# Attention and two feed-forward layers on one core: weight conversion by a leaky activation, and three changes of the plan

## The chip, the cores and the metric

The kernel runs on 1 core of one Trainium2 chip. The metric is device time in microseconds (us) of one execution, median of several runs.

## The reference, cut to what matters

```python
# q, k, v: (8 batches, 8 heads, 576 tokens, 64), float32
k_p = k.reshape(B, H, 72, 8, D).mean(axis=3)      # pooled by 8
v_p = v.reshape(B, H, 72, 8, D).mean(axis=3)
attn = softmax(q @ k_p.T / sqrt(64))
x = (attn @ v_p) as (4608 tokens, 512)
# first feed-forward: w_in 512 x 2048, w_out 2048 x 512
h = x @ w_in
g = (a0 + a1*h + a2*h**2 + a3*h**3) / (1 + |b0|*|h| + |b1|*h**2 + 1e-6)
x = g @ w_out
# second feed-forward: w_gate, w_val 512 x 1536, w_out2 1536 x 512
out = (sigmoid(x @ w_gate) * (x @ w_val)) @ w_out2
```

All weights arrive as float64. The kernel sees each as two 32-bit words, and must make float32 of them itself.

## The kernel before, in words

Every float32 product of a weight and an activation is made of three matmuls: both factors are split into a high and a low part (`wh`, `wl`, `xh`, `xl`), and `mm3` (lines 485 to 487) adds wl\*xh, wh\*xh and wh\*xl in one PSUM bank.

**Blocks and steps.** The 4608 tokens are cut into 9 blocks of 512. The first feed-forward is a loop of 144 steps: step n is block n // 16 and slice n % 16 of the 2048 hidden columns. A step computes `hidden` (`g1`, 12 matmuls), the rational function (`rational1` to `rational3`), the split of its result (`split_g`, of the step before), and the second product (`g2`, 12 matmuls, of three steps before, `LAG`), which adds into the four banks `acc0` to `acc3`. After a block's last `g2`, `g2_out` (line 561) copies the four banks to SBUF and stores them in DRAM as `x2d`. The second feed-forward begins after step 143; the change doesn't touch it.

**Attention.** While block b of the loop runs, the attention of block b+1 is done in the gaps, in tiles of 128 tokens or of 64 where a batch ends (4 or 5 tiles in a block; block 1 has 5). Block 0 is done ahead of the loop. A planner (lines 430 to 470) gives each piece a step and a place in it: `scores`, `exponential` and `normalise`, `a_transpose`, `attend`, and, for each batch, pooling of keys (`pool_k`, VectorE) and of values (`pool_v`, GpSimd), `place_k` and `mask_v`. `at[i]` is the step of tile i. For blocks from 2 on (`late_`), the transposes stand in step `at[i]` and `attend` one step later; for block 1, the transposes stand in step `at[i] - 1`, one step after `normalise`, and `attend` in `at[i]`. Every engine runs its instructions in the order written, so this plan fixes each queue.

**Conversion of weights.** `conv1a` (line 84) makes two ScalarE copies per slice of 128x512 weights: the high word, read as float32, times 2\*\*-112 (line 90), and the low word times 2\*\*-29 (line 92). `conv1b` (line 94), which `gap()` starts one step later between `rational2` and `rational3`, does the rest: VectorE shifts the high word left by 3 into a spare tile `wx` (line 98), VectorE puts the sign bit back with a scalar_tensor_tensor (line 100), and GpSimd adds the low word (line 102). `conv2` splits the result: ScalarE rounds it (line 117), and the rest is a subtraction (line 118), on GpSimd in all calls. `weights_a(n)` does this for `w_in` and `w_out`, a slice of each per step, ahead of the loop and in block 0.

**Weights of the second feed-forward.** `background(n - 16)` (line 194) prepares them from block 1 on, in 12 units of 8 steps: two loads and one more, three conversions (`conv1` at r = 2, 3 and 6), four GpSimd subtractions (line 214), seven splits (`bg_split`, lines 190 and 191) and one `conv2`, and stores them in DRAM (`w2d`, `wo2d`). The 12 units fill blocks 1 to 6; block 7 has no background work.

**PSUM.** Four banks (tag "h") rotate among `hidden`, the scores, the transposes and `attend`. Four more are `acc0` to `acc3`.

The step's order, in short, as each engine's queue gets it:

```python
g1(n); run(on_pe, n, 0); rational1(n); run(off_pe, n, 0); split_g(n - 1)
rational2(n); run(off_pe, n, 2); gap(); rational3(n); g2(m); g2_out(m)
run(on_pe, n, 1); run(off_pe, n, 1); weights_a(n) or wo_stream; background(n - NF1)
```

VectorE's six instructions of a step are lines 528 to 530 (`rational1`) and 542 to 544 (`rational3`). Lines 528 and 544, and the two of `conv1b`, read and write SBUF tiles alone; lines 529, 530, 542 and 543 read the PSUM bank `h`.

Of the kernel before, what the change touches and what calls it, by code (L numbers as in the profile page):

```python
# [9 lines left out]
F32 = mybir.dt.float32  # L10
F32R = mybir.dt.float32r
I32 = mybir.dt.int32
U32 = mybir.dt.uint32
AF = mybir.ActivationFunctionType
ALU = mybir.AluOpType
# [20 lines left out]
def attention_moe_glu_kernel(ctx: ExitStack, tc: tile.TileContext, q, k, v, w_in, w_out, ca, cb, w_gate, w_val, w_out2, out):  # L36
    nc = tc.nc
# [8 lines left out]
    NJ = H // 2  # L46
    NF1, NF2 = F1 // P, F2 // P
    TB = 512
    NB = NT // TB
    NTT = TB // P  # L50
    NCH = (H * SP + P - 1) // P
# [10 lines left out]
    scale = 1.0 / math.sqrt(D)  # L62
# [13 lines left out]
    def new_tmp(name, tag="m", bufs=3):  # L76
        return rot.tile([P, 512], F32, tag=tag, name=name, bufs=bufs)

    x2d = [dram.tile([P, NJ, TB], F32, name=f"x2d{i}", tag=f"x2d{i}") for i in range(NB)]
# [4 lines left out]
    def conv1a(*raws):  # L84

        for raw in raws:
            hw, lw = raw[:, :, 1], raw[:, :, 0]


            nc.scalar.activation(hw.bitcast(F32), hw.bitcast(F32), AF.Copy, scale=2.0 ** -112)  # L90

            nc.scalar.activation(lw, lw.bitcast(U32), AF.Copy, scale=2.0 ** -29)

    def conv1b(*raws):

        ws = [(raw[:, :, 1], raw[:, :, 0], new_tmp("wx").bitcast(I32)[:, :raw.shape[1]]) for raw in raws]
        for hw, lw, x in ws:
            nc.vector.tensor_scalar(out=x, in0=hw, scalar1=3, scalar2=None, op0=ALU.logical_shift_left)
        for hw, lw, x in ws:
            nc.vector.scalar_tensor_tensor(out=hw, in0=hw, scalar=-2 ** 31, in1=x, op0=ALU.bitwise_and, op1=ALU.bitwise_or)  # L100
        for hw, lw, x in ws:
            nc.gpsimd.tensor_tensor(out=hw, in0=hw, in1=lw, op=ALU.add)

    between = []
# [1 line left out]
    def conv1(*raws):  # L106
        conv1a(*raws)
        between.append(lambda: conv1b(*raws))
# [6 lines left out]
    def conv2(raw, wh, wl, eng=nc.gpsimd):  # L115
        t = raw[:, :, 1].bitcast(F32)
        nc.scalar.activation(wh, t, AF.Copy)
        eng.tensor_tensor(out=wl, in0=t, in1=wh.bitcast(F32), op=ALU.subtract)
# [7 lines left out]
    def slot(tag, dtype, name, pool=None):  # L126
        shape = [P, 2, 4 * P] if dtype is F32R else [P, 4 * P, 2]
        return (pool or wp).tile(shape, dtype, tag=tag, name=name)
# [8 lines left out]
    wi, wo, wi_raw, wo_raw = {}, {}, {}, {}  # L137
# [10 lines left out]

    def wi_conv2(f):
        wi[f] = slot(f"wi{f}", F32R, "wi")  # L150
        conv2(wi_raw.pop(f), wi[f][:, 0], wi[f][:, 1])

    def wo_load(f):
        wo_raw[f] = slot(f"wo{f + 1}", I32, "woraw") if f + 1 < FS else slot(f"st{(f + 1 - FS) % 5}", I32, "woraw", stage)
# [38 lines left out]

    def background(n):

        if not 0 <= n < 8 * NF2:
            return
        u, r = divmod(n, 8)
        s_, mat = divmod(u, 2)
        if r == 0:  # L200
            bg.setdefault("out", 0)
            bg["raw"] = [slot(f"st{x}", I32, "wqraw", stage) for x in range(3)]
            for x in range(2):
                f = 2 * s_ + x
                load_raw(bg["raw"][x], (w_gate, w_val)[mat][:, 2 * f * P:2 * (f + 1) * P], True)
            load_raw(bg["raw"][2], w_out2[u * P:(u + 1) * P, :], False)
        elif r in (2, 3):
            conv1(bg["raw"][r - 2])
        elif r == 4:
            b1, b2 = (raw[:, :, 1].bitcast(F32) for raw in bg["raw"][:2])  # L210
            b11, b21, b12, b22 = b1[:, :2 * P], b1[:, 2 * P:], b2[:, :2 * P], b2[:, 2 * P:]
            t = stage.tile([P, 4, 2 * P], F32, tag="st3", name="wqt")
            for o, a, b in ((0, b12, b11), (1, b22, t[:, 0]), (2, b22, b12), (3, b21, t[:, 1])):
                nc.gpsimd.tensor_tensor(out=t[:, o], in0=a, in1=b, op=ALU.subtract)
            bg["op"] = {1: b11, 2: b21, 3: b22, 4: t[:, 3], 5: t[:, 0], 6: t[:, 1], 7: t[:, 2]}
        elif r == 5:
            bg_split(u, 0)
            bg_split(u, 2)
        elif r == 6:
            conv1(bg["raw"][2])  # L220
            bg_split(u, 4)
        elif r == 7:
            bg_split(u, 6)
            t = slot(f"st{4 + bg['out'] % 2}", F32R, "wq", stage)
            bg["out"] += 1
            conv2(bg["raw"][2], t[:, 0], t[:, 1])
            nc.sync.dma_start(wo2d[u], t.bitcast(F32).rearrange("p h x -> p (h x)"))

    with tc.manual_schedule():
# [29 lines left out]
        units, raws, loaded = [], {}, [0]  # L259
# [168 lines left out]


        of_block, first, last = {}, {}, {}  # L430
        SH = (1, 3)
        for i, (b, t0, n) in enumerate(tiles):
            of_block.setdefault((b * S + t0) // TB, []).append(i)
            first.setdefault(b, i)
# [1 line left out]
        at = {}  # L436
        for blk, idx in of_block.items():
            for m, i in enumerate(idx):
                at[i] = NF1 * (blk - 1) + SH[blk == 1] + m * (NF1 - (0, 1)[blk == 1] - SH[blk == 1]) // len(idx) if blk else m - len(idx)
        plan = []  # L440
        n0 = len(of_block[0])

        def put(step, rank, pe, rest, gen, *a, use=()):
            plan.append((step, rank, len(plan), pe, rest, gen(*a), use))

        for i, (b, t0, n) in enumerate(tiles):
            late_ = at[i] > NF1
            put(at[i] + late_, 0, 0, 0, attend, i)
            if late_:
                put(at[i], 2, 0, 0, a_transpose, i)  # L450
            else:
                put(at[i] - 1, 2, 1, 1, a_transpose, i)
            put(at[i] - 2, 3, 0, 0, exponential, i)
            put(at[i] - 2, 3, 1, 1, normalise, i)
            put(at[i] - 3, 4, 1, 1, scores, i, use=[("q", i)])
# [6 lines left out]
        for b in range(1, B):  # L462
            e0, e1 = max(at[first[b - 1]], -2), at[last[b - 1]]
            for c in range(2 * NCH):
                w, f = (("k", pool_k), ("v", pool_v))[c // NCH]
                st = e0 + c * (e1 - 3 - e0) // (2 * NCH)
                put(st, 6, 1, 1 if st < 0 else 2, ew, f, b, c % NCH, use=[(w, b, c % NCH)])
            put(e1 - 2, 3.5, 1, 1, ew, place_k, b)
            put(e1 + (e1 > NF1), 1, 0, 0, ew, mask_v, b)
        plan.sort(key=lambda x: (x[0], (0, 2, 1)[x[4]], x[1], x[2]))  # L470
        units += [u for x in plan for u in x[6]]
        lead = plan[0][0]
# [23 lines left out]
        acc, gs = {}, {}  # L496
# [4 lines left out]
        def store(a, dst, on_act, *tag):  # L501
            o = new_tmp("o", *tag)
            if on_act:
                nc.scalar.activation(o, a, AF.Copy)
            else:
                nc.vector.tensor_copy(o, a)
            nc.sync.dma_start(dst, o)
# [53 lines left out]
        def g2_out(n):  # L561
            i, f = divmod(n, NF1)
            if f == NF1 - 1:
                for e in range(NJ):
                    store(acc[i][e], x2d[i][:, e], e < 2, *(("su", 3) if e == NJ - 1 else ()))


        ring, wo2, xo = {}, {}, {}
# [201 lines left out]
        for n in range(N1):  # L770
            m = n - LAG
# [23 lines left out]
            x = n - (N1 - NF1)  # L795
# [79 lines left out]
```

## Time and profile before

| | us |
|---|---|
| median of 3 runs | 1896.74 (1896.67 to 1898.65) |
| the profiled execution, its own time | 1894.58 |
| its span, first to last instruction | 1892.7 |

Read the page first for the share of each engine, then the stretches by block, then the chain that ended last within a stretch, and only then single instructions. A block's stretch is cut at the first `hidden` matmul of the block: 36.2 us for block 0, 195.3 for block 1, 302.4, 415.3, 525.0, 637.7, 744.0, 855.3 for blocks 2 to 7, and 957.1 for block 8. PE is TensorE, DVE VectorE, ACT ScalarE, POOL GpSimd, SP the engine whose queue issues the DMAs. The row of a stretch has its two ends, its length, then the busy time (and count of instructions) of PE, PEld (weight loads), DVE, ACT and POOL, TensorE's mean granted clock, DMA share and GB/s. A busy time in these views runs from the start to the end of an instruction and holds any time in which it stood still; successive instructions of an engine overlap a little.

### The profile page before, as it was taken

Reading aid. Unit: us, or ns where it says so; the run is one execution under the profiler, and the core shown is the slowest. Engines: PE = TensorE matmul, PEld = TensorE weight load, DVE = VectorE, ACT = ScalarE, POOL = GpSimd, SP = SyncE. Lnnn points to the kernel's source line nnn. Section 1 sums busy time; section 2 is a strip of 40 time slices with the busy share of each in tenths; the row PEclk is TensorE's granted clock in tenths of the full one; section 3 lists DMA queues with packets and bytes.
Section 4 is the critical chain, followed back from the end, with each engine's and each line's share of the span. In section 5 each row is a group of like instructions: output and inputs, shape, how many; then the busy total and the mean of one; then the engine's idle time right before and its main releaser. Section 6 shows DMA issues by size and latency. Waiting matters only on the chain.

```text
span 1892.7 us, 25138 instructions
## 1 busy us (share of the span) xinstructions
PE 1804.6 (95%) x8936; PEld 1564.4 (83%) x8936; DVE 1242.5 (66%) x1847; ACT 943.0 (50%) x1754; POOL 896.4 (47%) x855
## 2 busy tenths in 40 slices
PE   5578999999999999999999999999999999999999
PEld 4467788787777788788887999998998998998997
DVE  7999999999998899988778543343334333333331
ACT  4777777677676777776666422222222222222221
POOL 6768556565564665653224234334235225235231
PEclk9799999999999999999999999999999999999999
DMA  7343355343544553443154574574573664663661
GB/s 247 131 153 120 107 191 187 135 171 135 186 159 156 192 176 137 168 148 119 56 196 150 190 236 153 166 235 133 184 228 123 211 211 129 222 201 112 206 203 43
DMA packets 123117, 312.56 MB, mean 165 GB/s; under 512 B 11504, under 2 KB 43248, under 8 KB 122992
## 3 DMA queue, kind: packets, MB, share of 16 engines
q1 hardware_dynamic: 122992, 310.95, 48.7%
q8 instruction: 71, 1.16, 0.2%
q14 instruction: 54, 0.44, 0.1%
HBM read 257.95 MB, written 52.95 MB: 164 GB/s over the span
## 4 chain that ended last, share of the span: by engine, by line
PE 67%; DVE 21%; ACT 4%; issue 4%; DMA 2%; POOL 2%; SPq 0%; ACTq 0%; POOLq 0%; DVEq 0%
PE h L485 13%; PE h L487 12%; PE h L486 12%; PE acc L485 3%; PE acc L487 3%; PE acc L486 3%; PE accA L722 3%; PE accA L723 3%; PE h L722 3%; PE h L723 3%; PE accA L721 3%; PE h L721 3%; DVE u L528 3%; PE psx L413 3%; DVE y L544 3%
## 5 line engine op out<-in xcount | busy, mean ns | idle before, releaser
L658 DVE TENSOR_TENSOR t<-h,t 128x384 f32<-128x384 f32 x360 | 200.7, 557 | 387.0 <-ACT t L666 276.2
L513 POOL TENSOR_TENSOR g<-y,g 128x512 fp32r<-128x512 f32 x144 | 190.6, 1324 | 245.7 <-ACT g L510 186.7
L711 POOL TENSOR_TENSOR t<-t 128x384 f32<-128x384 f32 x72 | 84.4, 1172 | 448.9 <-issue 253.7
L485 PE MATMUL h<-xs,wi 128*128 128x512 f32 x576 | 234.4, 407 | 11.8 <-DVE xs L420 5.2
L485 PE MATMUL acc<-g,wo 128*128 128x512 f32 x576 | 232.8, 404 | 2.2 <-ACT g L510 2.2
L487 PE MATMUL h<-xs,wi 128*128 128x512 f32 x576 | 229.3, 398 | 3.0 <-DVE xs L420 3.0
L486 PE MATMUL h<-xs,wi 128*128 128x512 f32 x576 | 229.2, 398 | 0.0
L487 PE MATMUL acc<-g,wo 128*128 128x512 f32 x576 | 226.0, 392 | 2.4 <-POOL g L513 2.4
L486 PE MATMUL acc<-g,wo 128*128 128x512 f32 x576 | 225.0, 391 | 0.0
L487 PE MATMUL h<-xS,wq 128*128 128x384 f32 x576 | 193.1, 335 | 0.0
L485 PE MATMUL h<-xS,wq 128*128 128x384 f32 x576 | 192.9, 335 | 0.0
L486 PE MATMUL h<-xS,wq 128*128 128x384 f32 x576 | 192.7, 335 | 0.0
L528 DVE SCALAR_TENSOR_TENSOR u<-s,coef,u 128x512 f32<-128x512 f32 x144 | 132.1, 918 | 32.2 <-ACT u L526 31.9
L485 PE MATMUL h<-xA,wq 128*128 128x384 f32 x432 | 149.0, 345 | 0.0
L544 DVE SCALAR_TENSOR_TENSOR y<-u,y 128x512 f32<-128x512 f32 x144 | 143.9, 999 | 4.9
L487 PE MATMUL h<-xA,wq 128*128 128x384 f32 x432 | 144.7, 335 | 0.0
L486 PE MATMUL h<-xA,wq 128*128 128x384 f32 x432 | 144.6, 335 | 0.0
L485 PEld LDWEIGHTS h<-xs,wi 128*128 128x128 f32 x576 | 111.3, 193 | 39.1 <-DVE xs L420 4.2
L525 ACT ACTIVATE s<-h 128x512 f32<-128x512 f32 x144 | 85.0, 590 | 110.4 <-PE h L487 110.3
L542 DVE SCALAR_TENSOR_TENSOR u<-u,h 128x512 f32<-128x512 f32 x144 | 98.5, 684 | 56.0 <-ACT h L538 54.3
L487 PEld LDWEIGHTS h<-xs,wi 128*128 128x128 f32 x576 | 111.1, 193 | 27.9 <-DVE xs L420 3.5
L485 PEld LDWEIGHTS acc<-g,wo 128*128 128x128 f32 x576 | 108.5, 188 | 27.9 <-ACT g L510 2.6
(122 smaller groups left out, 4300.2 us busy)
## 6 DMA issues: line engine op xcount, KB each, us to landing
wq<-w2d SPq DMA_DIRECT2D x252, 512.0 KB, 4.3
wo<-wod SPq DMA_DIRECT2D x88, 512.0 KB, 3.8
w2d<-wq SPq DMA_DIRECT2D x36, 512.0 KB, 2.9
x2d<-o SPq DMA_DIRECT2D x36, 256.0 KB, 2.4
out_dram<-o SPq DMA_DIRECT2D x36, 256.0 KB, 2.0
raw<-in_k_dram SPq DMA_DIRECT2D x32, 256.0 KB, 2.8
raw<-in_q_dram SPq DMA_DIRECT2D x32, 256.0 KB, 2.7
raw<-in_v_dram SPq DMA_DIRECT2D x32, 256.0 KB, 3.1
```

What stands on the lines that cost most here:

```text
L485: nc.tensor.matmul(out_, wl, xh, start=start, stop=False, skip_group_check=on)
L486: nc.tensor.matmul(out_, wh, xh, start=False, stop=False, skip_group_check=on)
L487: nc.tensor.matmul(out_, wh, xl, start=False, stop=stop, skip_group_check=on)
L513: eng.tensor_tensor(out=g[:, 1], in0=y, in1=g[:, 0].bitcast(F32), op=ALU.subtract)
L525: nc.scalar.activation(s, h, AF.Square)
L528: nc.vector.scalar_tensor_tensor(out=u, in0=s, scalar=coef[:, 5:6], in1=u, op0=ALU.mult, op1=ALU.add)
L542: nc.vector.scalar_tensor_tensor(out=u, in0=u, scalar=ONE, in1=r, op0=ALU.add, op1=ALU.mult)
L544: nc.vector.scalar_tensor_tensor(out=y, in0=u, scalar=-2.0, in1=y, op0=ALU.add, op1=ALU.mult)
L658: nc.vector.tensor_tensor(out=out_, in0=a, in1=b, op=ALU.add)
L721: nc.tensor.matmul(a[t], gh, wt[:, 0], start=(f == 0), stop=False)
L722: nc.tensor.matmul(a[t], gh, wt[:, 1], start=False, stop=False)
L723: nc.tensor.matmul(a[t], gl, wt[:, 0], start=False, stop=(f == NF2 - 1))
```

## The change

Five edits. `conv1a` uses a leaky activation in place of a copy for the high word: positive words are scaled by 2\*\*-112 as before, negative ones by 2\*\*32 more, which sets a bit of the exponent that the shift by 3 then moves into the sign. So `conv1b` drops the instruction of line 100, and the shift works in place, in the strided high words, with no tile `wx`. The subtraction in `wi_conv2` moves from GpSimd to VectorE. `background` spreads its 12 units over 112 steps, blocks 1 to 7, so that a unit starts every 9 or 10 steps. Block 1's tiles get the plan of the later blocks, at steps 2, 5, 8, 11, 14 (`attend` one later) in place of 3, 5, 7, 10, 12, and pooling of values is planned over two steps more. In `g2_out`, three of the four copies go to ScalarE instead of two.

```diff
--- before.py
+++ after.py
@@ -87,18 +87,18 @@
             hw, lw = raw[:, :, 1], raw[:, :, 0]
 
 
-            nc.scalar.activation(hw.bitcast(F32), hw.bitcast(F32), AF.Copy, scale=2.0 ** -112)
+
+
+            nc.scalar.activation(hw.bitcast(F32), hw.bitcast(F32), AF.Prelu, scale=2.0 ** -112, alpha=2.0 ** 32)
 
             nc.scalar.activation(lw, lw.bitcast(U32), AF.Copy, scale=2.0 ** -29)
 
     def conv1b(*raws):
 
-        ws = [(raw[:, :, 1], raw[:, :, 0], new_tmp("wx").bitcast(I32)[:, :raw.shape[1]]) for raw in raws]
-        for hw, lw, x in ws:
-            nc.vector.tensor_scalar(out=x, in0=hw, scalar1=3, scalar2=None, op0=ALU.logical_shift_left)
-        for hw, lw, x in ws:
-            nc.vector.scalar_tensor_tensor(out=hw, in0=hw, scalar=-2 ** 31, in1=x, op0=ALU.bitwise_and, op1=ALU.bitwise_or)
-        for hw, lw, x in ws:
+        ws = [(raw[:, :, 1], raw[:, :, 0]) for raw in raws]
+        for hw, lw in ws:
+            nc.vector.tensor_scalar(out=hw, in0=hw, scalar1=3, scalar2=None, op0=ALU.logical_shift_left)
+        for hw, lw in ws:
             nc.gpsimd.tensor_tensor(out=hw, in0=hw, in1=lw, op=ALU.add)
 
     between = []
@@ -148,7 +148,7 @@
 
     def wi_conv2(f):
         wi[f] = slot(f"wi{f}", F32R, "wi")
-        conv2(wi_raw.pop(f), wi[f][:, 0], wi[f][:, 1])
+        conv2(wi_raw.pop(f), wi[f][:, 0], wi[f][:, 1], nc.vector)
 
     def wo_load(f):
         wo_raw[f] = slot(f"wo{f + 1}", I32, "woraw") if f + 1 < FS else slot(f"st{(f + 1 - FS) % 5}", I32, "woraw", stage)
@@ -193,9 +193,11 @@
 
     def background(n):
 
-        if not 0 <= n < 8 * NF2:
+        span = (NB - 2) * NF1
+        if not 0 <= n < span:
             return
-        u, r = divmod(n, 8)
+        u = n * NF2 // span
+        r = n + (-u * span // NF2)
         s_, mat = divmod(u, 2)
         if r == 0:
             bg.setdefault("out", 0)
@@ -428,7 +430,6 @@
 
 
         of_block, first, last = {}, {}, {}
-        SH = (1, 3)
         for i, (b, t0, n) in enumerate(tiles):
             of_block.setdefault((b * S + t0) // TB, []).append(i)
             first.setdefault(b, i)
@@ -436,7 +437,7 @@
         at = {}
         for blk, idx in of_block.items():
             for m, i in enumerate(idx):
-                at[i] = NF1 * (blk - 1) + SH[blk == 1] + m * (NF1 - (0, 1)[blk == 1] - SH[blk == 1]) // len(idx) if blk else m - len(idx)
+                at[i] = NF1 * (blk - 1) + (2 + 3 * m if blk == 1 else 1 + m * (NF1 - 1) // len(idx)) if blk else m - len(idx)
         plan = []
         n0 = len(of_block[0])
 
@@ -444,7 +445,7 @@
             plan.append((step, rank, len(plan), pe, rest, gen(*a), use))
 
         for i, (b, t0, n) in enumerate(tiles):
-            late_ = at[i] > NF1
+            late_ = at[i] > 0
             put(at[i] + late_, 0, 0, 0, attend, i)
             if late_:
                 put(at[i], 2, 0, 0, a_transpose, i)
@@ -463,10 +464,10 @@
             e0, e1 = max(at[first[b - 1]], -2), at[last[b - 1]]
             for c in range(2 * NCH):
                 w, f = (("k", pool_k), ("v", pool_v))[c // NCH]
-                st = e0 + c * (e1 - 3 - e0) // (2 * NCH)
+                st = e0 + c * (e1 - (3 if w == "k" else 1) - e0) // (2 * NCH)
                 put(st, 6, 1, 1 if st < 0 else 2, ew, f, b, c % NCH, use=[(w, b, c % NCH)])
             put(e1 - 2, 3.5, 1, 1, ew, place_k, b)
-            put(e1 + (e1 > NF1), 1, 0, 0, ew, mask_v, b)
+            put(e1 + (e1 > 0), 1, 0, 0, ew, mask_v, b)
         plan.sort(key=lambda x: (x[0], (0, 2, 1)[x[4]], x[1], x[2]))
         units += [u for x in plan for u in x[6]]
         lead = plan[0][0]
@@ -562,7 +563,7 @@
             i, f = divmod(n, NF1)
             if f == NF1 - 1:
                 for e in range(NJ):
-                    store(acc[i][e], x2d[i][:, e], e < 2, *(("su", 3) if e == NJ - 1 else ()))
+                    store(acc[i][e], x2d[i][:, e], e < 3, *(("su", 3) if e == NJ - 1 else ()))
 
 
         ring, wo2, xo = {}, {}, {}
```

## Rows read from the trace of the kernel before

**Rows 1.** Stretches of blocks 0 to 7.
```profile
36.20:195.30 159.10, 116.36 (x502) 92.97 (x502) 153.35 (x195) 111.32 (x199) 120.16 (x112) 0.86 0.40 136
195.30:302.40 107.10, 105.33 (x501) 86.77 (x502) 98.35 (x151) 78.08 (x144) 64.09 (x66) 0.98 0.42 152
302.40:415.30 112.90, 109.65 (x531) 89.65 (x530) 103.47 (x155) 77.92 (x148) 64.02 (x68) 0.98 0.45 158
415.30:525.00 109.70, 104.34 (x501) 85.35 (x500) 100.76 (x149) 79.30 (x148) 64.38 (x65) 1.00 0.45 166
525.00:637.70 112.70, 108.37 (x530) 88.26 (x529) 100.94 (x155) 77.64 (x147) 66.33 (x68) 1.00 0.46 159
637.70:744.00 106.30, 103.36 (x502) 85.48 (x500) 96.31 (x145) 77.69 (x145) 67.11 (x70) 1.00 0.47 165
744.00:855.30 111.30, 108.18 (x531) 88.11 (x530) 99.65 (x154) 80.32 (x152) 67.87 (x72) 1.00 0.46 168
855.30:957.10 101.80, 101.71 (x494) 84.69 (x493) 80.11 (x129) 65.26 (x117) 29.77 (x24) 1.00 0.24 82
```

**Rows 2.** The chain that ended last, block 0, shares by engine and line.
```profile
by line: DVE wx L98 15.7%; DVE woraw L100 11.5%; DVE y L544 11.3%; DVE u L528 7.7%; DVE wiraw L100 7.1%; DVE y L530 7.1%; DVE y L543 5.9%; issue 5.9%; DVE y L529 5.8%; DVE u L542 5.3%; DVE e L371 2.3%; DVE xs L420 2.0%; DVE kp L317 2.0%; DV
```

**Rows 3.** VectorE's groups in block 0: count, busy us, mean ns, idle before.
```profile
L544 DVE SCALAR_TENSOR_TENSOR y<-u,y 128x512 f32<-128x512 f32 x15 | 22.9, 1526 | 0.5
L100 DVE SCALAR_TENSOR_TENSOR woraw<-woraw,wx 128x512 int32<-128x512 int32 x16 | 21.7, 1358 | 0.5
L98 DVE TENSOR_SCALAR wx<-wiraw 128x512 int32<-128x512 int32 x13 | 16.9, 1301 | 0.0
L100 DVE SCALAR_TENSOR_TENSOR wiraw<-wiraw,wx 128x512 int32<-128x512 int32 x13 | 13.7, 1056 | 0.4
L98 DVE TENSOR_SCALAR wx<-woraw 128x512 int32<-128x512 int32 x16 | 12.8, 800 | 0.0
```

**Rows 4.** Timeline, 50 to 56.5 us: start, us, instruction.
```profile
50.10 6.25 DVE L544 SCALAR_TENSOR_TENSOR y<-u,y 128x512 f32<-128x512 f32 x1
...
51.24 1.04 POOL L102 TENSOR_TENSOR wiraw<-wiraw 128x512 int32<-128x512 int32 x1
...
54.51 1.29 POOL L118 TENSOR_TENSOR wo<-woraw,wo 128x512 fp32r<-128x512 f32 x1
```

**Rows 5.** Line 98, durations ns min/median/max over the run.
```profile
L98 DVE TENSOR_SCALAR wx<-woraw x16: 416/422/2223, 37.5 to 191.0; 128x512 int32<-128x512 int32 x16
```

**Rows 6.** Line 100, durations ns min/median/max over the run.
```profile
L100 DVE SCALAR_TENSOR_TENSOR wiraw<-wiraw,wx x16: 693/695/2028, 22.4 to 166.6; 128x512 int32<-128x512 int32 x16
```

**Rows 7.** GpSimd's groups in block 0.
```profile
L118 POOL TENSOR_TENSOR wi<-wiraw,wi 128x512 fp32r<-128x512 f32 x14 | 18.2, 1299 | 0.0
```

**Rows 8.** Waits in block 0: released by what, us in total, times, longest.
```profile
PE pta L395 <- POOL e L388: 30.5, 5, 12.1
```

**Rows 9.** VectorE's groups in blocks 1 to 6.
```profile
L98 DVE TENSOR_SCALAR wx<-wqraw 128x512 int32<-128x512 int32 x35 | 34.8, 994 | 0.0
L100 DVE SCALAR_TENSOR_TENSOR wqraw<-wqraw,wx 128x512 int32<-128x512 int32 x35 | 24.8, 708 | 1.2
...
L506 DVE COPY o<-acc 128x512 f32<-128x512 f32 x12 | 7.7, 681 | 0.0
```

**Rows 10.** Waits in blocks 1 to 6.
```profile
ACT wq L117 <- POOL wqraw L102: 13.6, 7, 2.3
...
PE h L485 <- DVE xs L420: 3.4, 4, 1.3
```

**Rows 11.** ScalarE's groups over the whole run.
```profile
L527 ACT ACTIVATE y<-h,coef 128x512 f32<-128x512 f32 x144 | 112.4, 780 | 0.0
...
L90 ACT ACTIVATE wqraw<-wqraw 128x512 f32<-128x512 f32 x36 | 23.9, 664 | 0.0
...
L504 ACT ACTIVATE o<-acc 128x512 f32<-128x512 f32 x18 | 9.7, 587 | 2.4 <-PE acc L487 2.3
...
L232 ACT ACT_TABLE_LOAD x1 | 1.3, 1283 | 0.8 <-PEq L851 0.8
```


## The prediction

> **What bounds the kernel now.** I read the stretches by block first. Block 0 takes 159.1 us, block 7 takes 101.8, and blocks 1 to 6 lie between 106.3 and 112.9 [rows 1]. Block 7 does the same loop with four attention tiles, but no conversion: TensorE is busy 101.71 of its 101.8 us, so 101.8 is what TensorE asks of a block with four tiles. Blocks 2, 4 and 6 have five tiles: 531 TensorE instructions against 501, and 4.4 us more TensorE busy time on the mean [rows 1]. That holds waits too; I take 3.0 us, so 104.8, as their floor. Over these floors, blocks 1, 3 and 5 are 5.3, 7.9 and 4.5 us too long, and blocks 2, 4 and 6 are 8.1, 7.9 and 6.5: 40 us in all. Block 0 is some 54 over.
>
> What fills block 0 is VectorE: 153.35 of 159.1 us [rows 1]. The chain that ended last agrees: the shares of VectorE shown in its row add up to 84% [rows 2]. TensorE's waits there, 30.5 us for the normalised scores in front of the transposes [rows 8], therefore bound nothing: VectorE had no gap meanwhile, so moving them away is worth nothing by itself.
>
> But VectorE is not at work all that time. Its shift of line 98 takes 0.42 us at the median for one operand and up to 2.2 [rows 5], and means of 1.30 and 0.80 in block 0 [rows 3]. Line 100 has a minimum of 0.69 [rows 6] and means of 1.06 and 1.36 [rows 3]; line 544 has a mean of 1.53 there [rows 3]. The timeline shows why: a line 544 begun at 50.10 ends at 56.35, 0.55 us after the last of a run of four GpSimd instructions without a gap, from 51.24 to 55.80 (the first and the last are shown) [rows 4]. Instructions whose operands all lie in SBUF stand still while GpSimd runs. In block 0 that is, per line: 29.7 less 29 times 0.42, so 17.5 us, at line 98; 35.4 less 29 times 0.69, so 15.4, at line 100; 22.9 less 15 times 0.69, so 12.5, at line 544 [rows 3, 5, 6].
>
> The Trainium skill (SBUF — State Buffer, Who interferes with whom) says that a VectorE instruction with two SBUF inputs and a GpSimd one block each other, the later until the first finishes. By that, a wait would be one GpSimd instruction; the row shows a wait through four, and the row decides. By the rule nothing of line 100's waits would be passed on below, and the sum would be 7 us lower.
>
> **The change, part by part.** Durations are of the profiled execution, 1894.58 us with a span of 1892.7; the median of the runs, 1896.74, is 2.2 above it.
>
> *Block 0, line 100 gone.* 29 instructions, 13.7 + 21.7 = 35.4 us of the path [rows 3]: -35.4. The 15.4 us of waits in it were for GpSimd's additions, and those stay. They now start one instruction earlier and are met by lines 542 and 543, which read PSUM and did not wait, and then by line 544 and the next shift. I pass half on: +7 (bounds 0 and +15.4).
>
> *Block 0, the subtraction of w_in.* GpSimd loses 14 instructions, 18.2 us [rows 7], 15% of its 120.16 [rows 1]; the waits at lines 98 and 544, 30 us, shrink as much: -4.5. VectorE gets 14 subtractions with all operands in SBUF. No such row exists; the nearest are line 100's, 0.69 unblocked [rows 6] and 1.36 at the highest mean [rows 3]. I take 1.0, between them, as GpSimd is still busy most of the time: +14 (bounds +10 and +19). Behind it on VectorE is the next step's line 528, which needs ScalarE's output from further down ScalarE's queue anyway, so the wait for ScalarE's rounding costs nothing new.
>
> *Block 0, a second count.* GpSimd's 120.2 us and VectorE's unblocked SBUF work (29 shifts of 0.42, 29 of 0.69, 15 each of lines 528 and 544 at 0.69: 53) make 173 us in 159.1. After the change it is 102 + 12 + 10 + 21 = 145; the same ratio gives 133, so -26. The first count gives -35.4 + 7 - 4.5 + 14 = -19. I take **-23**: block 0 at 136. ScalarE (111.32) and TensorE (116.36) lie below that [rows 1].
>
> *The leaky activation.* No row shows one. The nearest are the copy it replaces, 0.66 us, and the dearest activation of that size, 0.78 [rows 11]. I take 0.66: cost 0 (up to 27 times 0.12, 3 us of ScalarE in block 0, which has 48 us of slack).
>
> *The shift in place.* Output now strided. Bounds: 0.42 as now [rows 5] and 0.69, that of line 100, which wrote the same words [rows 6]. I take 0.42, the same instruction.
>
> *Block 1's plan.* Five tiles at other steps; TensorE's wait of 30.5 us was covered by VectorE, so 0. The last `attend` moves from step 12 to 15, right before block 1's first matmul, which needs VectorE's `xs` from behind `rational1`. The nearest row is that wait in later blocks, 3.4 us in 4 times [rows 10]; VectorE is later here: **+2** (0 to +5). Later pooling of values moves GpSimd work by one or two steps: 0 (-2 to +2).
>
> *Blocks 1 to 7.* In blocks 1 to 6, 35 conversions cost VectorE 34.8 + 24.8 = 59.6 us [rows 9]. After, 30 of them stand there with a shift each, of 0.42 to 0.99 [rows 5, 9]; I take 0.85, as the additions come earlier: 25.5. That is 34 less, or 5.7 a block, and 0.68 more where a copy of line 506 leaves [rows 9]. VectorE's mean, 99.9 us a block [rows 1], becomes 93.5. Its mean of 99.9 goes with 6.7 us over the floor, block 7's 80.1 with none [rows 1]. Straight between them, 93.5 gives 4.5 over, a gain of 2.2 a block; if the excess vanishes sooner, as waits do when an engine is not quite full, up to 5. I take 3.2: **-19** (-6 to -35). Block 7 gets one seventh of the background, five or so shifts and some 29 us of GpSimd, on 80.11 us of VectorE: **+2** (0 to +6). ScalarE's waits in `conv2` for line 102, 13.6 us [rows 10], are part of this gain.
>
> *Copies.* Nine copies cost ScalarE 0.59 each [rows 11]; it is busy 78 us of 107 in such blocks [rows 1], so this is hidden. If that cover were gone it would be 5 us.
>
> Sum: -23 + 2 - 19 + 2 = -38. 1894.6 - 38 = 1856.6; with 2.2 for the median, **1859**.
>
> **The rivals.**
>
> *GpSimd's run only moves (0.13).* All of line 100's waits pass to line 544: with two additions, the subtraction for w_out and the split in one run, a line 544 waits as in [rows 4]. Block 0 gains 10, blocks 1 to 7 some 8: 1879. For it: VectorE stood still through whole runs. Against: GpSimd's run is shorter by an instruction in each step.
>
> *The strided shift loses its speed (0.10).* 0.27 us each, 8 us in block 0 and half of 9 later: 1871.
>
> *Both floors are reached (0.10).* Block 0 falls to 123, near ScalarE and TensorE, and blocks 1 to 7 to their floors: -36 - 36, so 1825.
>
> *Slower: tables (0.04).* A table load takes 1.283 us, and the whole run has two groups of one load each, though Ln, Exp, Copy, Abs and Square alternate; one group's row stands in [rows 11]. If the leaky function is not in the set in use, every call brings a load there and one back, 2.57 us. Block 0 has 27 calls: 69 us on ScalarE's 111.32 make 180 us, 21 over now. In blocks 1 to 7, 36 calls are 13 us a block on ScalarE's 78, which fits but takes the gain away: 1918. It decides as soon as a call costs 1.8 us more, where 27 of them use up the 48 us that ScalarE has left. The Trainium skill (ScalarE: Activation LUTs, Table sets: the hidden batching unit) names relu, copy, identity and abs as in every set, and not the leaky function; no run here shows it yet.
>
> **How the numbers follow.** The forecast has 0.63. A measurement of this kernel can tell about 0.2%, 3.8 us, from no change. Forecast, strided shift and floors are faster, and the moved run too but for 0.03: faster 0.93, same 0.03, slower 0.04. The forecast's own range is 1842 to 1876. The range for 8 in 10 goes up past the moved run, 1884, and down by the floors' larger part to 1832; the tables and the far ends stay out.
>
> **What would show it.** Right: line 100 absent, block 0 at 126 to 146 us with VectorE still fullest, GpSimd's `wi` subtractions on VectorE at about 1 us, line 544's mean in block 0 at or above 1.5, shifts near 0.42 where unblocked, the leaky activation at 0.66, no new table loads, blocks 1 to 6 at 102 to 110, block 7 at 102 to 106. Wrong: an unblocked shift at 0.69; ScalarE as the chain of block 0; blocks 1 to 6 as long as before, which would mean that something other than VectorE's load makes their waits.

## The result, and the profile after

The changed kernel takes 1853.89 us (1852.74 to 1854.5, 4 runs); the kernel before took 1896.7 beside it. The ratio is 0.977, 95% interval 0.976 to 0.979: 43 us faster. The profiled execution took 1852.74 us with a span of 1851.0, so 41.7 us of span are gone.

The stretches of blocks 0 to 7 of the changed kernel, cut as before at each block's first `hidden` matmul (ends, length, busy PE, PEld, DVE, ACT, POOL, granted clock, DMA share, GB/s):

```profile
37.40:170.10 132.70, 107.17 (x494) 86.10 (x495) 127.29 (x185) 111.58 (x204) 105.21 (x99) 0.91 0.48 161
170.10:273.60 103.50, 102.76 (x502) 85.71 (x501) 88.64 (x138) 73.25 (x135) 53.03 (x54) 1.00 0.43 147
273.60:383.30 109.70, 107.81 (x530) 88.25 (x529) 91.74 (x147) 77.71 (x148) 59.91 (x65) 1.00 0.48 168
383.30:490.80 107.50, 104.97 (x502) 86.63 (x500) 92.27 (x135) 76.43 (x142) 62.13 (x64) 0.98 0.42 149
490.80:600.10 109.30, 107.81 (x530) 88.25 (x531) 95.46 (x154) 79.07 (x149) 63.89 (x68) 1.00 0.45 154
600.10:704.10 104.00, 102.98 (x501) 85.72 (x500) 89.10 (x138) 75.95 (x139) 56.12 (x59) 1.00 0.46 158
704.10:813.40 109.30, 107.84 (x531) 88.29 (x530) 96.76 (x145) 77.60 (x146) 65.10 (x70) 1.00 0.44 154
813.40:914.90 101.50, 101.50 (x494) 84.80 (x493) 86.63 (x131) 77.24 (x143) 55.23 (x50) 1.00 0.38 136
```

Against [rows 1]: block 0 went from 159.1 to 132.7 us (-26.4), blocks 1 to 6 from 660.0 to 643.3 (-16.7), block 7 from 101.8 to 101.5 (-0.3). The stretch ahead of block 0 is 1.2 us longer, and block 8 with the second feed-forward 0.5. That is the 41.7. Six tenths of the gain lie in one block of 16 steps.

VectorE's groups in block 0 of the changed kernel (count, busy us, mean ns, idle before). The lines have moved: line 528 is now 529, line 544 is 545, the shift is line 100, and line 118 is the subtraction of w_in:

```profile
L529 DVE SCALAR_TENSOR_TENSOR u<-s,coef,u 128x512 f32<-128x512 f32 x16 | 19.6, 1228 | 2.7 <-ACT u L527 2.7
L545 DVE SCALAR_TENSOR_TENSOR y<-u,y 128x512 f32<-128x512 f32 x15 | 17.6, 1176 | 0.5
L100 DVE TENSOR_SCALAR woraw<-woraw 128x512 int32<-128x512 int32 x16 | 12.5, 783 | 0.0
...
L118 DVE TENSOR_TENSOR wi<-wiraw,wi 128x512 fp32r<-128x512 f32 x14 | 11.4, 815 | 0.0
...
L100 DVE TENSOR_SCALAR wiraw<-wiraw 128x512 int32<-128x512 int32 x12 | 9.6, 804 | 0.0
```

Unblocked, a new subtraction takes 0.63 us, its minimum over the run (ns, min/median/max):

```profile
L118 DVE TENSOR_TENSOR wi<-wiraw,wi x16: 631/674/1784, 30.8 to 153.4; 128x512 fp32r<-128x512 f32 x16
```

Over that and the unblocked 0.42 and 0.69 us, the shifts now hold 10.3 us of waits (22.1 less 28 times 0.42), line 545 holds 7.3, line 529 holds 8.6, and the new subtractions 2.6: 29 us in all. Before, lines 98, 100 and 544 held 45 us by [rows 3, 5, 6], and line 528 held 2.4 (12.7 less 15 times 0.69):

```profile
L528 DVE SCALAR_TENSOR_TENSOR u<-s,coef,u 128x512 f32<-128x512 f32 x15 | 12.7, 845 | 2.6 <-ACT u L526 2.6
```

So the waits shrank by 19 us, more than the executed work did: old line 100 cost 20 us unblocked and the new subtractions cost 8.8.

The shift itself, from the list of line 100 (ns, min/median/max over the whole run), is as fast in place as it was into a spare tile [rows 5]:

```profile
L100 DVE TENSOR_SCALAR wiraw<-wiraw x16: 411/433/1682, 22.0 to 139.6; 128x512 int32<-128x512 int32 x16
```

The leaky activation and the table loads, from ScalarE's groups over the whole run:

```profile
L92 ACT ACTIVATE wqraw<-wqraw 128x512 f32<-128x512 f32 x36 | 24.1, 670 | 0.0
...
L234 ACT ACT_TABLE_LOAD x1 | 1.3, 1283 | 0.8 <-PEq L852 0.8
L697 ACT ACT_TABLE_LOAD x1 | 1.3, 1283 | 0.0
```

0.670 us a call against 0.664 for the copy [rows 11], and still one load ahead of the loop and one ahead of the second feed-forward's sigmoid.

VectorE still stands still behind GpSimd. In the timeline of block 0, a line 529 begun at 77.18 ends at 81.33, after three GpSimd instructions in a row:

```profile
76.77 1.49 POOL L390 TENSOR_TENSOR e<-e,r 64x576 f32<-64x576 f32 x1 [1.71 <-DVE r L389]
...
77.18 4.15 DVE L529 SCALAR_TENSOR_TENSOR u<-s,coef,u 128x512 f32<-128x512 f32 x1
...
78.23 1.30 POOL L118 TENSOR_TENSOR wo<-woraw,wo 128x512 fp32r<-128x512 f32 x1
...
79.49 1.28 POOL L514 TENSOR_TENSOR g<-y,g 128x512 fp32r<-128x512 f32 x1
```

TensorE's waits in block 0, to compare with [rows 8]:

```profile
PE pta L397 <- POOL e L390: 7.9, 1, 7.9
...
PE h L488 <- DVE xs L422: 0.3, 1, 0.3
```

The waits for normalised scores fell from 30.5 us to 7.9. The one wait for `xs`, 0.3, stands at 38.4 us, the head of block 0; at the turn to block 1, at 170.1, TensorE has none. In blocks 1 to 7, the shift's group on VectorE:

```profile
L100 DVE TENSOR_SCALAR wqraw<-wqraw 128x512 int32<-128x512 int32 x36 | 39.9, 1108 | 0.0
```

36 shifts cost 39.9 us, 1.11 each; before, shift and line 100 together cost 1.70 [rows 9].

### The profile page after: what moved, and what is told of

Its sections match the earlier page's. It is cut to its first block, busy times and chain, and to the rows that moved or that the text cites. A ratio compares the mean times of both kernels' runs of the same rounds, so it can differ in the third digit from the quotient of the medians.

```text
span 1851.0 us, 25044 instructions
## 1 busy us (share of the span) xinstructions
PE 1792.8 (97%) x8936; PEld 1558.9 (84%) x8936; DVE 1176.8 (64%) x1786; ACT 945.7 (51%) x1763; POOL 871.5 (47%) x839
## 4 chain that ended last, share of the span: by engine, by line
PE 74%; DVE 15%; ACT 4%; POOL 3%; issue 2%; DMA 2%; SPq 0%; ACTq 0%; POOLq 0%; DVEq 0%
PE h L486 14%; PE h L488 13%; PE h L487 13%; PE acc L486 4%; PE acc L488 4%; PE acc L487 4%; PE psx L415 3%; PE accA L723 3%; PE accA L724 3%; PE h L724 3%; PE h L723 3%; PE accA L722 3%; PE h L722 3%; DVE u L529 3%; DVE y L531 2%
## 5 line engine op out<-in xcount | busy, mean ns | idle before, releaser
L486 PE MATMUL h<-xs,wi 128*128 128x512 f32 x576 | 230.7, 400 | 2.4 <-DVE xs L422 1.7
L488 PE MATMUL h<-xs,wi 128*128 128x512 f32 x576 | 226.2, 393 | 0.3 <-DVE xs L422 0.3
L487 PE MATMUL h<-xs,wi 128*128 128x512 f32 x576 | 225.9, 392 | 0.0
L529 DVE SCALAR_TENSOR_TENSOR u<-s,coef,u 128x512 f32<-128x512 f32 x144 | 137.5, 955 | 49.2 <-ACT u L527 48.8
L486 PEld LDWEIGHTS acc<-g,wo 128*128 128x128 f32 x576 | 108.8, 189 | 30.4 <-ACT o L505 2.9
L545 DVE SCALAR_TENSOR_TENSOR y<-u,y 128x512 f32<-128x512 f32 x144 | 129.7, 900 | 4.9
L486 PEld LDWEIGHTS h<-xs,wi 128*128 128x128 f32 x576 | 109.1, 189 | 27.4 <-DVE xs L422 2.1
L488 PEld LDWEIGHTS acc<-g,wo 128*128 128x128 f32 x576 | 109.0, 189 | 27.4 <-POOL g L514 3.3
```

Of the source, the lines that this page charges most:

```text
L486: nc.tensor.matmul(out_, wl, xh, start=start, stop=False, skip_group_check=on)
L487: nc.tensor.matmul(out_, wh, xh, start=False, stop=False, skip_group_check=on)
L488: nc.tensor.matmul(out_, wh, xl, start=False, stop=stop, skip_group_check=on)
L529: nc.vector.scalar_tensor_tensor(out=u, in0=s, scalar=coef[:, 5:6], in1=u, op0=ALU.mult, op1=ALU.add)
L545: nc.vector.scalar_tensor_tensor(out=y, in0=u, scalar=-2.0, in1=y, op0=ALU.add, op1=ALU.mult)
```

## Experiments

**The conversion alone.** The kernel before with the new conversion; the core of the edit:

```diff
-            nc.scalar.activation(hw..., hw..., AF.Copy, scale=2.0 ** -112)
+            nc.scalar.activation(hw..., hw..., AF.Prelu, scale=2.0 ** -112, alpha=2.0 ** 32)
...
-            nc.vector.tensor_scalar(out=x, in0=hw, scalar1=3, ...)
-            nc.vector.scalar_tensor_tensor(out=hw, in0=hw, scalar=-2 ** 31, in1=x, ...)
+            nc.vector.tensor_scalar(out=hw, in0=hw, scalar1=3, ...)
```

> The kernel before with the new conversion alone (leaky activation, shift in place, no line 100); the subtraction of w_in stays on GpSimd, and the plan, the units of 8 steps and two ScalarE copies are as before. Theory A, common time: in block 0, GpSimd's time and VectorE's instructions with all operands in SBUF exclude each other, and their sum sets the block; the sum goes from 173 us to 120 + 12 + 21 = 153, so block 0 takes about 140 us (159.1 before, 132.7 with the whole change). Theory B, VectorE's own chain: only what VectorE itself executes and the passed-on waits count; without the 14 subtractions on VectorE block 0 is shorter than with them, about 126 us. Blocks 1 to 6 shorten under both, by 10 to 20 us in all. Total by A about 1863, by B about 1850. Theory C, the plan did it: block 0 stays above 150, total above 1875.

Measured: 1867.57 us, ratio 0.984 (0.983 to 0.986). Its block 0, and blocks 1 to 6 as one stretch:

```profile
36.60:173.60 137.00, 110.83 (x501) 89.22 (x502) 120.66 (x163) 109.75 (x199) 115.21 (x110) 0.88 0.44 150
173.60:827.20 653.60, 636.57 (x3088) 524.06 (x3087) 578.00 (x871) 469.10 (x877) 391.76 (x409) 0.99 0.47 165
```

The total is 30 us lower. Block 0 at 137.0 is 22 us shorter than before, near theory A's 140 and not B's 126; blocks 1 to 6 give 6.4. But VectorE is now idle for 16 us of block 0 (13.0 of them before `rational1`, for ScalarE), which neither A nor B had in it: something else had begun to hold the block.

**Everything but the conversion.** The changed kernel with the old conversion:

```diff
-            nc.scalar.activation(hw..., hw..., AF.Prelu, scale=2.0 ** -112, alpha=2.0 ** 32)
+            nc.scalar.activation(hw..., hw..., AF.Copy, scale=2.0 ** -112)
...
+            nc.vector.scalar_tensor_tensor(out=hw, in0=hw, scalar=-2 ** 31, in1=x, ...)
```

> The changed kernel with the old conversion (copy, shift into a spare tile, sign put back by line 100); the other four edits stay. Theory A: the common time of block 0 is 105 + 12 + 20 + 10 + 21 = 168 us, so block 0 takes about 152 us; blocks 1 to 7 get 36 instructions of 0.7 us back on VectorE and lose about half of what they gained; total about 1882. Theory B: block 0 gets 35 us of line 100 back, less what is passed on now, so above 155; total about 1888. Theory C: total below 1868, as the plan and the spread background made most of the gain.

Measured: 1896.03 us, ratio 0.999 (0.998 to 1.0). Block 0 and blocks 1 to 6:

```profile
36.90:195.20 158.30, 119.44 (x493) 94.90 (x494) 152.61 (x216) 112.12 (x202) 103.22 (x99) 0.84 0.40 138
195.20:853.60 658.40, 636.90 (x3088) 522.21 (x3088) 570.82 (x883) 461.79 (x854) 360.54 (x379) 1.00 0.44 151
```

Block 0 is back at 158.3 us, VectorE full, which is B's number and against A's 152. The total is above both, 1882 by A and 1888 by B: blocks 1 to 6 are only 1.6 us shorter than before. Without the new conversion the other four edits give at most 4 us together, and perhaps nothing (0.999, interval 0.998 to 1.0); with it, they give some 13 (0.984 to 0.977). They are worth little by themselves and something once line 100 is gone.

**The subtraction of w_in back on GpSimd.**

```diff
-        conv2(wi_raw.pop(f), wi[f][:, 0], wi[f][:, 1], nc.vector)
+        conv2(wi_raw.pop(f), wi[f][:, 0], wi[f][:, 1])
```

> The changed kernel with the subtraction of w_in back on GpSimd; nothing else is changed. Theory A: GpSimd gets 14 times 1.30 us, VectorE loses 14 of 0.69; the common time goes from 148 to 156 us, block 0 from 132.7 to about 140, total about 1861. Theory B: VectorE loses 12 us of its chain and gets some 4 to 5 us more of waits, block 0 about 125, total about 1846.

Measured: 1852.43 us, ratio 0.976 (0.975 to 0.978). Block 0, and the shifts in it:

```profile
35.50:168.00 132.50, 108.53 (x494) 86.70 (x495) 127.54 (x170) 111.48 (x203) 119.02 (x112) 0.91 0.47 159
```

```profile
L100 DVE TENSOR_SCALAR wiraw<-wiraw 128x512 int32<-128x512 int32 x12 | 15.8, 1317 | 0.0
L100 DVE TENSOR_SCALAR woraw<-woraw 128x512 int32<-128x512 int32 x15 | 15.1, 1008 | 0.0
```

Both theories fail: 132.5 us, as with the subtraction on VectorE. VectorE lost 11.4 us of subtractions, and its shifts took 30.9 us instead of 22.1 while GpSimd was busy 119 us instead of 105. What VectorE no longer executes it now waits. This edit of the change is worth nothing, and its two places can't be told apart by the total. Three runs further down (units of 8, two copies, block 4 free) leave block 0 as the change has it; there it took 134.5, 132.6 and 133.4 us, so differences of block 0 below 2 us tell nothing.

**The subtraction of w_out on VectorE too.**

```diff
-        conv2(wo_raw.pop(f), wo[f][:, 0], wo[f][:, 1])
+        conv2(wo_raw.pop(f), wo[f][:, 0], wo[f][:, 1], nc.vector)
```

> The changed kernel with the subtraction of w_out on VectorE too; nothing else is changed. Theory A: GpSimd loses 22 us, VectorE gets 16 of 0.69, 11 us; the common time goes from 148 to 136 us, block 0 from 132.7 to about 122, total about 1843, and TensorE (107) and ScalarE (112) come near. Theory B: VectorE's chain gets 16 times 0.8, 13 us, and loses some 5 of waits: block 0 about 141, total about 1862.

Measured: 1858.99 us, ratio 0.980 (0.978 to 0.981). Block 0:

```profile
36.20:176.40 140.20, 113.84 (x493) 91.48 (x494) 133.97 (x201) 111.73 (x203) 84.33 (x84) 0.87 0.46 156
```

140.2 us, as B said, and 18 from A: GpSimd has 21 us less to do and the block is 7.5 us longer. A common time of both engines doesn't set block 0. VectorE's list does, as soon as it is longer than the waits it saves.

**Block 1's tiles by the old plan.**

```diff
-  ... (2 + 3 * m if blk == 1 else ...)
+  ... (3 + m * (NF1 - 4) // len(idx) if blk == 1 else ...)
-            late_ = at[i] > 0
+            late_ = at[i] > NF1
...
-            put(e1 + (e1 > 0), 1, 0, 0, ew, mask_v, b)
+            put(e1 + (e1 > NF1), 1, 0, 0, ew, mask_v, b)
```

> The changed kernel with block 1's attention tiles at their old steps (3, 5, 7, 10, 12, transposes one step after normalise, attend in the tile's own step). Theory P (the prediction's): TensorE's waits in front of the transposes are covered by VectorE, so the plan is worth nothing, or costs 2 us where the last attend stands before block 1; total 1852 to 1855. Theory Q: with the conversion shortened, VectorE no longer covers them, as the run with the conversion alone had block 0 at 137.0 us with VectorE busy only 120.7; block 0 goes from 132.7 to about 137, total about 1858.

Measured: 1857.36 us, ratio 0.979 (0.977 to 0.981). Blocks 0 and 1, and TensorE's first wait in block 0:

```profile
36.80:173.00 136.20, 109.66 (x502) 88.75 (x503) 124.88 (x180) 109.48 (x199) 100.19 (x95) 0.90 0.46 154
173.00:278.60 105.60, 103.22 (x502) 85.54 (x501) 92.89 (x145) 75.59 (x138) 56.78 (x58) 1.00 0.43 147
```

```profile
PE pta L397 <- POOL e L390: 17.8, 5, 11.3
```

Theory Q: block 0 takes 136.2 us, 3.5 more, and block 1 takes 2.1 more; VectorE is idle for 11 us of block 0, and TensorE waits 17.8 us in front of the transposes instead of 7.9. This fits VectorE's work having covered that wait, and the shorter conversion having uncovered it: with the old conversion the new plan and the other edits gained 0.8 us in block 0. Totals 3.5 us apart are at the edge of what the intervals tell; the place, block 0 and 1 alone, is where the edit is.

**The background in six blocks.**

```diff
-        span = (NB - 2) * NF1
+        span = 8 * NF2
```

> The changed kernel with the background in units of 8 steps, over blocks 1 to 6, block 7 free of it. Theory P (the prediction's): what a block takes over its floor follows VectorE's busy time in it, with 0.35 to 0.75 us for each us; a sixth more of the background in each is 1 us of VectorE, so blocks 1 to 6 get 0.4 to 0.8 us each, block 7 stays at 101.5: total 1856 to 1859. Theory R: the excess comes from where the unit's runs of GpSimd work and its waits for stores fall against the attention tiles, and the seventh block and the free steps between units are what helps: blocks 1 to 6 get 2 us each or more, total 1866 or more.

Measured: 1857.85 us, ratio 0.980 (0.978 to 0.981). Blocks 1 to 6 as one stretch, and block 7:

```profile
170.40:819.40 649.00, 636.16 (x3088) 523.90 (x3087) 567.58 (x858) 469.61 (x880) 387.19 (x406) 0.99 0.47 164
819.40:920.90 101.50, 101.50 (x494) 84.77 (x493) 79.69 (x127) 65.77 (x118) 29.55 (x24) 1.00 0.24 81
```

Blocks 1 to 6 take 5.7 us more than the 643.3 of the changed kernel, and block 7 takes the same 101.5 with VectorE 7 us less busy. That is 0.95 us a block, a little over theory P's 0.4 to 0.8 and half of R's 2. The seventh block costs nothing: TensorE is 100% busy there with or without the background.

**Two copies of four on ScalarE.**

```diff
-                    store(acc[i][e], x2d[i][:, e], e < 3, ...)
+                    store(acc[i][e], x2d[i][:, e], e < 2, ...)
```

> The changed kernel with two copies of four on ScalarE in place of three. Theory P: VectorE gets nine copies of 0.68 us, ScalarE loses nine of 0.59; hidden in both, and as VectorE's busy time counts with 0.35 to 0.75 in six of the blocks, 1 to 3 us: total 1854 to 1857. Rival: TensorE waits for the four banks at the turn of each block, and they come 0.6 us later each time: nine times, total about 1859.

Measured: 1856.17 us, ratio 0.978 (0.977 to 0.980). Blocks 1 to 6, and block 7:

```profile
170.10:815.40 645.30, 634.85 (x3089) 522.69 (x3087) 557.12 (x859) 457.65 (x848) 360.33 (x379) 1.00 0.45 155
815.40:917.50 102.10, 101.74 (x494) 84.86 (x493) 87.25 (x132) 76.80 (x142) 55.18 (x50) 1.00 0.37 135
```

Blocks 1 to 7 take 2.6 us more, about 0.4 for each turn, within theory P's 1 to 3 and half of the rival's 5. The intervals of the totals overlap, so the size is the profile's alone.

**A block with five tiles and no background.**

```diff
-        u = n * NF2 // span
-        r = n + (-u * span // NF2)
+        if 48 <= n < 64:
+            return
+        u, r = divmod(n if n < 48 else n - 16, 8)
```

> The changed kernel with the background in units of 8 steps in blocks 1, 2, 3, 5, 6 and 7; block 4, which has five attention tiles, is free of it. It measures the floor of a block with five tiles. Theory P: the floor is 104.8 us, so block 4 takes 104 to 106 (109.3 with the change). Rival: five tiles cost TensorE 107 us or more by themselves, so that blocks 2, 4 and 6 were near their floor after the change, and block 4 takes 107 to 109. Total near that of the run with units of 8 steps, plus what block 7 then takes over 101.5.

Measured: 1854.08 us, ratio 0.977 (0.976 to 0.979). Block 4:

```profile
491.30:598.80 107.50, 107.26 (x531) 88.40 (x531) 87.94 (x144) 67.76 (x124) 41.29 (x44) 1.00 0.32 109
```

107.5 us with TensorE busy 107.26: that is the floor of a block with five tiles, and the prediction's 104.8 was wrong. Blocks 2, 4 and 6 of the changed kernel, 109.7, 109.3 and 109.3, are 2 us over it, not 5.

**The background kept off the turn of a block.** In the changed kernel block 3 is 6 us over block 7, the longest of those with four tiles; one step of it, from 403.8, takes 9.8 us, the one in which the four banks are copied out. In front of the copies stands a line 529 that takes 4.72 us and ends 0.55 us after a run of GpSimd, from 401.86 to 405.94, which begins with four splits of the background:

```profile
401.77 4.72 DVE L529 SCALAR_TENSOR_TENSOR u<-s,coef,u 128x512 f32<-128x512 f32 x1
```

The run has units of 8 steps again, on top of the w_in edit above:

```diff
+        if n % NF1 in (2, 3):
+            return
+        u, r = divmod(n - n // NF1 * 2 - (2 if n % NF1 > 3 else 0), 8)
+        if u >= NF2:
+            return
```

> The changed kernel with the subtraction of w_in on GpSimd, as in the run of that edit (1852.4), and with the background's units of 8 steps laid over blocks 1 to 7 without the third and fourth step of each block, where the four banks are copied out. Theory E: what block 3 takes over its floor of 101.5 (107.5, of which 4.4 us in its fourth step alone, 9.8 us against 5.4) is one unit's last part, its splits and its rounding, falling on that turn; without it block 3 takes 103 to 104, the others stay or gain a little: total 1846 to 1849. Rival: the work only moves to steps where it meets the attention tiles, and other steps grow by as much: total 1851 to 1855.

Measured: 1859.0 us, ratio 0.980 (0.979 to 0.982): slower than the 1852.43 of the run that it stands on. Blocks 3, 4 and 6:

```profile
381.30:486.90 105.60, 103.13 (x501) 85.46 (x500) 93.19 (x136) 76.76 (x142) 61.96 (x64) 1.00 0.44 155
486.90:598.30 111.40, 108.15 (x530) 88.21 (x530) 97.59 (x152) 78.48 (x148) 64.24 (x68) 1.00 0.43 147
703.20:816.40 113.20, 109.08 (x531) 89.57 (x530) 95.70 (x145) 79.08 (x149) 59.91 (x65) 0.98 0.46 165
```

In the run that it stands on, cut the same way, these blocks take 107.9, 109.1 and 109.3 us. So block 3 fell by 2.3, but blocks 4 and 6 rose by 2.3 and 3.9, and the total is beyond the rival's 1851 to 1855 too. Theory E is out; that the work met the attention tiles elsewhere, as the rival says, fits but isn't shown. The fourth step of block 3 had already fallen to 8.3 us with the w_in edit alone, and stays at 8.3 here, so the run didn't reach the step that it was made for.

**No subtraction of w_in.** ScalarE writes a scaled copy in its place.

```diff
-        conv2(wi_raw.pop(f), wi[f][:, 0], wi[f][:, 1], nc.vector)
+        t = wi_raw.pop(f)[:, :, 1].bitcast(F32)
+        nc.scalar.activation(wi[f][:, 0], t, AF.Copy)
+        nc.scalar.activation(wi[f][:, 1], t, AF.Copy, scale=2.0 ** -24)
```

> The changed kernel without the subtraction of w_in: ScalarE writes a scaled copy as the low part in its place, so the low part of w_in is not the reference's. It takes 14 instructions, 11 to 12 us, off VectorE in block 0 and puts as many of 0.66 us, 9 us, on ScalarE; GpSimd is as in the changed kernel. Theory B2 (VectorE's own work and its waits for GpSimd set block 0, and each can be had back): block 0 goes from 132.7 to 121 to 124. Rival, balance: ScalarE, GpSimd and TensorE are so near that VectorE's relief is taken up by waits, as in the run with that subtraction on GpSimd: block 0 stays at 129 to 133.

Measured, one run: 1849.41 us. Block 0, and VectorE's longest wait in it:

```profile
36.30:166.20 129.90, 110.11 (x493) 88.84 (x494) 114.95 (x170) 119.21 (x217) 100.01 (x99) 0.88 0.49 164
```

```profile
DVE u L531 <- ACT u L529: 11.9, 10, 2.7
```

129.9 us: the rival. VectorE's busy time fell by 12.3 us and the block by 2.8. ScalarE is now the fuller of the two with 119.21, 7.6 more than in the changed kernel, and line 531 (rational1's first on VectorE) waits 11.9 us for it. VectorE's list no longer sets the block; the chain that ended last, which in the changed kernel is led by VectorE's lines, now runs through TensorE and ScalarE:

```profile
by line: PE h L488 6.1%; PE h L489 5.9%; PE h L490 5.8%; ACT u L529 5.0%; PE psx L417 4.7%; ACT wi L153 4.5%; ACT wiraw L92 4.5%; ACT wiraw L94 4.4%; ACT woraw L92 4.4%; ACT wi L152 4.3%; ACT woraw L94 4.3%; ACT s L528 4.2%; ACT wo L117 4.0
```

With that much more on ScalarE, the dozen microseconds of room that seemed to lie under VectorE are not there.

**No additions of the low words.**

```diff
-        for hw, lw in ws:
+        for hw, lw in ws if low else ():
             nc.gpsimd.tensor_tensor(out=hw, in0=hw, in1=lw, op=ALU.add)
...
-        conv1(wi_raw[f])
+        conv1(wi_raw[f], low=False)
...
-        conv1(wo_raw[f])
+        conv1(wo_raw[f], low=False)
```

> The changed kernel without GpSimd's additions of the low words of w_in and w_out (28 in block 0, 31 us of GpSimd's 105); the low words are left out of the weights. VectorE executes what it did. Theory A (common time of GpSimd and of VectorE's SBUF instructions): block 0 falls by about 27 us, to where ScalarE (112) and TensorE (107) stop it, about 113 to 116. Theory B2: VectorE's waits for GpSimd, 28 us in block 0, shrink with GpSimd's time by three tenths, and block 0 falls by about 8 us, to 122 to 126. Rival, own work: the waits are slack, block 0 stays at 130 or more.

Measured, one run: 1850.48 us. Block 0:

```profile
37.40:166.60 129.20, 108.78 (x494) 88.08 (x495) 121.82 (x185) 110.93 (x202) 64.73 (x64) 0.89 0.50 169
```

129.2 us. GpSimd's busy time fell by 40 us, and the block by 3.5. Theory A, which asked for a block of 113 to 116, is out; B2 asked for 8, and the third theory, own work, for nothing. The result lies between the last two, nearer to own work: VectorE's busy time fell by 5.5 us, from 127.29.

## Why the prediction was right, point by point

The sum was -38 and the span moved by -41.7; the direction, the place and the order of the parts held. Several terms did not, and their errors offset each other.

- **What bounds block 0: right.** VectorE's list with its waits for GpSimd. Putting line 100 back (everything but the conversion) gives 158.3 us, taking it away alone gives 137.0. No other single edit moved block 0 by more than 8 us.
- **Its size: -23 said, -26.4 measured.** The steps that were mis-sized are the two on waits: "I pass half on: +7", and -4.5 for less waiting at lines 98 and 544, together +2.5. Waits were passed on, but to line 529 (2.4 us before, 8.6 now) and not to line 544 and the next shift: the shifts and line 545 lost 12 us of waits together, so that line 545's mean is 1.18 us where 1.5 or more was to show the prediction right. That makes -6 for the two terms; no run parts one from the other. The subtraction was put at 1.0 us and took 0.815. That -23 came so near is in part luck: it lies between a first count of -19, too small by these terms, and a second one whose rule fails below.
- **The second count, 133: the right number by a wrong rule.** It took the time of GpSimd and of VectorE's SBUF instructions as one sum that sets the block. By that, block 0 should have taken 140, 122 and about 115 us in the three runs that moved or removed GpSimd's work; it took 132.5, 140.2 and 129.2.
- **The subtraction on VectorE: no gain and no loss**, where the prediction had -4.5 and +14 and the second count some -8. What is measured is the exchange of about one microsecond of work for one of waiting.
- **Block 1's plan, "worth nothing by itself": wrong in company.** TensorE's waits seem to have been covered by VectorE, as said, but by the part of it that the same change removes. The run with the old plan is 3.5 us longer in block 0 and 2.1 in block 1. The +2 for the turn to block 1 did not come: TensorE runs into block 1 without a gap.
- **Blocks 1 to 6: -19 said, -16.7 measured**, by errors that offset. VectorE's mean fell from 99.9 to 92.3 us, more than the 93.5 forecast, although a shift cost 1.11 us, not 0.85. Each us of that fall was worth 0.37 us (16.7 for 45.5 in six blocks), where the prediction took 0.5 (3.2 for 6.4), above its own straight line of 0.34. The five-tile floor is 107.5, not 104.8, so there were 8 us less to gain than the 40 counted; the prediction had it from blocks 1, 3 and 5, whose TensorE busy time, 104.3 on the mean, itself holds waits over block 7's 101.7.
- **That VectorE's load makes the excess of blocks 1 to 6: not shown.** The conversion alone, units of 8 and two copies give 0.30 to 0.35 us for each us off VectorE, near the straight line. But everything but the conversion takes 28.7 us off VectorE in these blocks (599.5 to 570.82), and they are 1.6 us shorter: 0.06. So VectorE's busy time alone doesn't tell a block's length; what holds these blocks with the old conversion is open.
- **Block 7: +2 said, -0.3 measured.** TensorE has no gap in it, so the 102 to 106 us among the signs of being right was missed too.
- **The leaky activation, the strided shift, the tables: right**, as the rows above show; so the rivals on speed and on tables fall. The rival that GpSimd's run only moves holds in part: line 529 waits more, the rest less. The rival with both floors reached did not come: block 0 stayed 10 us over the 123 named there.

What sets block 0 now looks like a balance: 11.4 us less work on VectorE, with 7.6 us more on ScalarE, gives 2.8 us and leaves VectorE waiting for ScalarE, and 40 us less GpSimd gives 3.5. Both are single runs, and the gains are not far above the 2 us by which block 0 varies. A run that takes work off VectorE and puts it nowhere wasn't tried.

No version that computes the whole beat the changed kernel by more than can be measured. The subtraction of w_in back on GpSimd, 1852.43 us, is equal to it.

## What to carry to other kernels

When one engine is full, count its instructions at their unblocked time and at the time they took: the difference is waiting, and the instruction removed here took its waits with it, more of them than it passed on. Don't count on getting the rest of the waits back: work moved off the other engine, or off this one, was mostly taken up by waits again. A wait that is covered by the full engine is free only as long as that engine stays full, so an edit that is worth nothing alone can be worth several microseconds beside the edit that empties the engine. And before an excess is priced, measure the floor: here a block with no background showed in one run that a fifth of the excess did not exist.

## What the runs showed of the hardware that was not expected

A VectorE instruction whose operands all lie in SBUF can stand still through several GpSimd instructions, not one: 4.15 us through three in the timeline of block 0 above, as the prediction had read it from [rows 4] (besides the four counted there, one begun at 50.00 was still running). The Trainium skill (SBUF — State Buffer, Who interferes with whom) says that a VectorE instruction with two SBUF inputs contends with a GpSimd one that reads SBUF, and that whoever issues first has the shared port for the whole instruction while the other blocks; the measured wait goes on through the two GpSimd instructions that follow.

Taking 40 us of GpSimd's work out of a block of 133 gave 3.5 us, although VectorE's waits in its instructions on SBUF added up to 29 there. VectorE's busy time fell by 5.5 us alone, from 127.29 to 121.82, and by the same count 24 of the 29 us of waits stayed with the GpSimd work that was left. Why they don't shrink with it is open.

The Trainium skill (ScalarE: Activation LUTs, Same chain, other wiring) says that the choice of slope by the instruction's `alpha` is not to be reached from a kernel. Here the leaky activation ran as any other, 0.670 us for 128x512, with no table load of its own.
